# Clamping and scaling an MLP's h on VectorE straight from PSUM, and exponentials per head with bias and row sum

## The chip, the cores and the metric

One core of one Trainium2 chip runs the whole program. The metric is the device time of one execution in microseconds (us), the median of several runs. Engines: TensorE (PE, its weight loads are PEld), VectorE (DVE), ScalarE (ACT), GpSimd (POOL), and SyncE (SP), which issues the DMA transfers.

## What is computed

Three stages in float32, each feeding the next.

```python
# pooled attention: q, k, v are 8 x 8 x 576 x 64 (batch, heads, tokens, features)
k_p = k.reshape(B, H, 72, 8, D).mean(axis=3); v_p = ...      # 72 pooled keys and values
scores = q @ k_p.T / sqrt(D)
attn = exp(scores - max(scores)); attn = attn / (sum(attn) + 1e-09)
x = (attn @ v_p)  ->  4608 tokens x 512
# first MLP
h = x @ w_in                                                  # 512 -> 2048
g = where(h >= 1, h, where(h <= -1, 0, (h + 1)**2 / 4))
x = g @ w_out                                                 # 2048 -> 512
# second MLP: h = x @ w_in2; g = h * sigmoid(h); out = g @ w_out2
```

## The kernel before

Every product of the large matrices is made of float16 parts: an operand is scaled by a power of two and split into a high and a low half, and `three` (L119 to L122) issues the three products high x high, high x low and low x high into one PSUM bank. The scales are taken from the data while the program runs, so there are many operations of one column on DVE.

**The first MLP.** The 4608 tokens are 9 tiles of 512 (`NTILE`, `N`), the 2048 hidden features 16 chunks of 128 (`KF`). For a chunk, `emit_h` (twelve matmuls) makes h as 128 features x 512 tokens in one PSUM bank, `hps`. The pool `ps_h` has two banks; in the first tile four of every six chunks borrow one of the four `ps_y` banks instead. Four steps then make g:

- `pre_A` (L801, ACT): Relu of c1 x h + br from PSUM into an SBUF tile `g`
- `min_A` (L93 through the helper `ts`, DVE): the minimum of that with `lim`, into `u`
- `mid_A` (L808, ACT): the square of `u`, scaled
- `post_A` (L812, DVE): the larger of `g` - br and `u`, into `g`

`split_g` makes the halves for the next product: a cast on ACT (L840) and a subtraction on DVE (L841). The tiles `g` and `u` have three buffers each (`up`). `consts_A` works out c1, br, lim and the other factors of a tile from the scale of its x. The chunks of the weights (nine pieces, `cuts1`) have scales of their own, so c1 differs between pieces. `emit_yA` multiplies g with the second weight, three chunks behind h (`LAG`), into the four `ps_y` banks; `evac_yA` takes those out through ACT and DVE (L93 with `y`).

**The first tile is different.** Its 16 chunks of g are kept ("stash"), while the second weight W2 is still being converted in four column blocks: read as words and rebuilt in float32 on ACT and DVE (`xf`, L174 and others), its largest value found, scaled by a factor `ws` (ACT L207), cast (ACT L212), and the low half subtracted (POOL L213). Then all 16 chunks are multiplied with one column block after the other. The factor `ws` is computed on DVE. The looks at the first weight (L239, L240) stand in the same way ahead of the first h.

**The attention** runs in 36 tiles of 128 tokens, one tile ahead of the MLP. For a tile `att_qT` scales and splits the rows of q (mean L443, split L359 on ACT and L360 on DVE; the result is `rows`) and a DMA transposes them (`qT`). `att_scores` makes scores of 128 tokens x 8 heads x 72 keys in two PSUM banks (`att`, L542), four heads in each; then, half by half, DVE takes the maximum over 72 keys (L556) and subtracts it (L557) into an SBUF tile `e`, and one ACT instruction takes the exponential of all 576 columns (L561) with `scale` = `cq`, one number per token. The first four tiles run in float32 with a constant scale. `att_norm` sums e on DVE (L576), adds a small number (L577), takes the reciprocal (L580), multiplies on POOL (L581) and splits into halves. `att_T` transposes, and `att_pv` multiplies with the values and splits x (`xh`, `xl`). Keys and values are pooled by `kv_pool` on DVE (L438), eight sums for each batch of 576 tokens.

**What sets the order.** The source is written in the order of the loops shown below, with a chunk's parts one step behind each other. The order on each engine is then made by the Tile framework's scheduler, which simulates a timeline when the program is built; `paced` and `tc.issue_after` tie weight work to other instructions, and `tc.high_priority` draws the attention forward. So an edit in one place can move instructions elsewhere. Tiles of a pool are reused in turn: an instruction that writes one waits for the last reader of its former content.

The second MLP follows, from 957 us in the profile below, in blocks of 256 tokens with seven products instead of eight (`group_B`); the diff doesn't touch it.

## Time and profile before

| | |
|---|---|
| median of 3 runs | 1643.12 us (1642.25 to 1645.21) |
| profiled execution, span | 1642.1 us |
| instructions | 34714 |
| PE busy | 1552.3 us (95%) |
| DVE busy | 1267.9 us (77%) |
| ACT busy | 895.4 us (55%) |
| POOL busy | 536.1 us (33%) |

The profiled execution's own time is its span, 1642.1 us, 1.0 us under the median of the runs. Busy shares are means over the whole span. The program has stages: until the first h it loads and looks at weights; then the first tile without its second product; then the main loop; and at last the second MLP. So the share to look at is that of a stage, and for a wait the instruction that ends it.

### The profile page before, as it was taken

How to read it: one execution, taken by the hardware profiler on the slowest of the kernel's cores; microseconds unless marked ns; L12 is line 12 of the kernel's file. 1: busy time of each engine (PE TensorE's matmuls, PEld its weight loads, DVE VectorE, ACT ScalarE, POOL GpSimd, SP SyncE). 2: the span in 40 equal slices, each digit the busy share in tenths (PEclk: the TensorE clock that was granted, in tenths of full speed). 3: DMA queues.
4: the chain of work that ended last, by engine and by line, in shares of the span. 5: the costliest groups of instructions: out<-in, count | busy, mean ns of one | idle time of the engine just before them, and what ended most of it. 6: DMA issues, size and time to landing. Idle time of an engine off the chain costs nothing.

```text
span 1642.1 us, 34714 instructions
## 1 busy us (share of the span) xinstructions
PE 1552.3 (95%) x14406; PEld 1075.0 (65%) x14406; DVE 1267.9 (77%) x2208; ACT 895.4 (55%) x1420; POOL 536.1 (33%) x479
## 2 busy tenths in 40 slices
PE   6886799899999999999999999999999999999998
PEld 5642344444444444444444479999999999999998
DVE  6898887879888697887767667777677777777765
ACT  5477454665657557475656554555444554545543
POOL 2221512131323323231445423433343433343322
PEclk8687999999999999999999999999999999999999
DMA  9454468744445445357474330000100001000000
GB/s 292 117 172 101 104 152 219 175 107 123 133 114 152 87 129 127 77 140 213 156 298 136 147 129 28 27 28 28 40 27 27 28 33 35 27 27 28 27 15 27
DMA packets 217086, 166.36 MB, mean 101 GB/s; under 512 B 153952, under 2 KB 176480, under 8 KB 216928
## 3 DMA queue, kind: packets, MB, share of 16 engines
q1 hardware_dynamic: 216928, 164.14, 35.4%
q8 instruction: 113, 1.85, 0.5%
q14 instruction: 45, 0.37, 0.1%
HBM read 102.76 MB, written 33.55 MB: 83 GB/s over the span
## 4 chain that ended last, share of the span: by engine, by line
PE 40%; DVE 26%; issue 11%; ACT 9%; DMA 8%; POOL 6%; SPq 1%; DVEq 0%; ACTq 0%; POOLq 0%
DVE sum L438 5%; POOL c L702 4%; PE y L120 3%; PE y L122 3%; PE y L121 3%; PE y L1002 3%; PE y L1004 3%; PE y L1003 3%; PE hb L121 3%; PE hb L120 3%; PE hb L122 3%; PE hps L122 3%; PE hps L120 3%; PE hps L121 3%; DVE g L812 3%
## 5 line engine op out<-in xcount | busy, mean ns | idle before, releaser
L121 PE MATMUL hb<-xl,wc 128*128 128x128 f16 x2016 | 347.6, 219 | 0.0
L120 PE MATMUL hb<-xh,wc 128*128 128x128 f16 x2016 | 347.6, 219 | 0.0
L122 PE MATMUL hb<-xh,wc 128*128 128x128 f16 x2016 | 347.6, 219 | 0.0
L360 DVE SCALAR_TENSOR_TENSOR g<-c,tsg,g 128x512 f16<-128x512 f32 x252 | 228.6, 910 | 93.7 <-ACT g L359 93.7
L1002 PE MATMUL y<-wd,g 128*128 128x256 f16 x1008 | 274.7, 273 | 1.0 <-DVE ob L1015 1.0
L1003 PE MATMUL y<-wd,g 128*128 128x256 f16 x1008 | 274.7, 273 | 0.0
L1004 PE MATMUL y<-wd,g 128*128 128x256 f16 x1008 | 274.7, 273 | 0.0
L942 ACT ACTIVATE c<-c,tc 128x512 f32<-128x512 f32 x144 | 103.2, 717 | 229.8 <-DVE c L939 229.8
L359 ACT ACTIVATE g<-c,tsg 128x512 f16<-128x512 f32 x252 | 177.6, 718 | 85.7 <-POOL c L705 48.3
L120 PE MATMUL hps<-xh,wa 128*128 128x512 f16 x576 | 222.1, 386 | 2.2 <-ACT g L801 1.8
L120 PE MATMUL y<-g,wb 128*128 128x512 f16 x544 | 209.2, 387 | 15.6 <-ACT wb L212 11.5
L121 PE MATMUL hps<-xl,wa 128*128 128x512 f16 x576 | 221.8, 385 | 2.0 <-DVE skv L95 2.0
L122 PE MATMUL hps<-xh,wa 128*128 128x512 f16 x576 | 220.7, 384 | 0.0
L122 PE MATMUL y<-g,wb 128*128 128x512 f16 x544 | 210.2, 386 | 4.1 <-POOL wb L213 3.9
L121 PE MATMUL y<-g,wb 128*128 128x512 f16 x544 | 210.3, 386 | 0.7 <-DVE g L841 0.5
L939 DVE TENSOR_TENSOR c<-c,hb 128x512 f32<-128x512 f32 x252 | 168.0, 681 | 43.1 <-PE hb L122 40.9
L121 PEld LDWEIGHTS <-wc 128*128 128x128 f16 x2016 | 197.3, 98 | 2.4
L120 PEld LDWEIGHTS <-wc 128*128 128x128 f16 x2016 | 197.3, 98 | 2.2
L122 PEld LDWEIGHTS <-wc 128*128 128x128 f16 x2016 | 197.3, 98 | 0.0
L702 POOL TENSOR_TENSOR c<-c 128x512 f32<-128x512 f32 x108 | 164.0, 1532 | 2.8
L808 ACT ACTIVATE u<-u,trsg 128x512 f32<-128x512 f32 x144 | 103.3, 718 | 100.6 <-DVE u L93 100.4
L581 POOL TENSOR_TENSOR e<-e,den 128x576 f32<-128x576 f32 x36 | 44.4, 1237 | 348.2 <-DVE den L580 248.0
(185 smaller groups left out, 2802.4 us busy)
## 6 DMA issues: line engine op xcount, KB each, us to landing
raw<-in_moe_w_out_dram SPq DMA_DIRECT2D x21, 1024.0 KB
raw<-in_moe_w_in_dram SPq DMA_DIRECT2D x18, 1024.0 KB
raw<-in_v_dram SPq DMA_DIRECT2D x32, 288.0 KB
y<-y SPq DMA_DIRECT2D x36, 256.0 KB
yin<-y SPq DMA_DIRECT2D x18, 512.0 KB
out_dram<-ob SPq DMA_DIRECT2D x36, 256.0 KB
d<-hl SPq DMA_DIRECT2D x32, 256.0 KB
raw<-in_k_dram SPq DMA_DIRECT2D x28, 288.0 KB
```

The lines of the kernel that those rows point to most:

```text
L120: nc.tensor.matmul(out=acc, lhsT=wh, rhs=xh, start=start, stop=False)
L121: nc.tensor.matmul(out=acc, lhsT=wh, rhs=xl, start=False, stop=False)
L122: nc.tensor.matmul(out=acc, lhsT=wl, rhs=xh, start=False, stop=stop)
L359: a = nc.scalar.activation(out=hi, in_=x, func=AF.Copy, scale=s)
L360: return a, nc.vector.scalar_tensor_tensor(out=lo, in0=x, scalar=s, in1=hi, op0=ALU.mult, op1=ALU.subtract)
L702: nc.gpsimd.tensor_tensor(out=out, in0=a, in1=b, op=ALU.subtract)
L808: nc.scalar.activation(out=u_t[s], in_=u_t[s], func=AF.Square, scale=r["rsg"])
L939: nc.vector.tensor_tensor(out=out, in0=x, in1=y, op=ALU.add)
L942: nc.scalar.activation(out=x, in_=x, func=AF.Silu, scale=r["c1"])
L1002: nc.tensor.matmul(out=acc, lhsT=xh, rhs=wh, start=start, stop=False)
L1003: nc.tensor.matmul(out=acc, lhsT=xh, rhs=wl, start=False, stop=False)
L1004: nc.tensor.matmul(out=acc, lhsT=xl, rhs=wh, start=False, stop=stop)
```

## The change

Softmax: `att_scores` no longer subtracts. The maximum of a half is multiplied by -scale on DVE (two columns of four numbers each, a small `ts`), and ACT takes the exponential of each head's 72 columns straight from PSUM, with that product as `bias`, `scale` as before, and with `accum_out` writing the row's sum into `den`. There are eight such instructions for a tile where there was one. The sum on DVE in `att_norm` is gone.

First MLP: `pre_A` is now a DVE instruction that reads h from PSUM and clamps it between two numbers per partition, `lim` and its negative, which depend on the piece of the weight. `min_A` is gone. `mid_A` squares with a scale `cs` per piece and the bias `br`. `post_A` takes h from PSUM once more, multiplies it by c1 and takes the larger of that and the square. So ACT's Relu is gone, the two DVE instructions read PSUM, and the bank of h is read last by `post_A`, where before it was by `pre_A`. `consts_A` works out `cs`, `rs` and `lim` (18 columns) instead of `rsg` and a single `lim`.

```diff
--- before.py
+++ after.py
@@ -498,7 +498,7 @@
             done += n
         return r
 
-    q_t, qT_t, cq_t, at_t, aT_t, kT = {}, {}, {}, {}, {}, {}
+    q_t, qT_t, cq_t, at_t, aT_t, kT, den_t = {}, {}, {}, {}, {}, {}, {}
 
     def load_q(i):
         if i == NI - 1:
@@ -551,14 +551,17 @@
 
         e = at_t[i] = ap.tile([128, H, SP], F32, tag="e", name="e", bufs=2)
         mx = sm.tile([128, H], F32, tag="mx", name="mx")
+        den = den_t[i] = sm.tile([128, H], F32, tag="den", name="den")
+        scale = cq_t.pop(i, 1.0 / (POOL * D ** 0.5))
         for hf, sv in enumerate(halves):
             m4 = mx[:, 4 * hf:4 * hf + 4]
             nc.vector.tensor_reduce(out=m4, in_=sv, axis=AX.X, op=ALU.max)
-            nc.vector.tensor_tensor(
-                out=e[:, 4 * hf:4 * hf + 4], in0=sv, in1=m4.unsqueeze(2).to_broadcast([128, 4, SP]),
-                op=ALU.subtract,
-            )
-        nc.scalar.activation(out=e, in_=e, func=AF.Exp, scale=cq_t.pop(i, 1.0 / (POOL * D ** 0.5)))
+            ts(m4, m4, scale, -1.0, ALU.mult, ALU.mult)
+            for h in range(4 * hf, 4 * hf + 4):
+                nc.scalar.activation(
+                    out=e[:, h], in_=sv[:, h % 4], func=AF.Exp, scale=scale, bias=mx[:, h:h + 1],
+                    accum_out=den[:, h:h + 1],
+                )
 
     late = {}
 
@@ -572,8 +575,7 @@
 
     def att_norm(i):
         e = at_t[i]
-        den = sm.tile([128, H], F32, tag="den", name="den")
-        nc.vector.tensor_reduce(out=den, in_=e, axis=AX.X, op=ALU.add)
+        den = den_t.pop(i)
         nc.vector.tensor_scalar(
             out=den, in0=den, scalar1=1e-9, scalar2=2.0 ** -14, op0=ALU.add, op1=ALU.mult
         )
@@ -620,7 +622,8 @@
     def att_pv(i):
         t, j = divmod(i, NI)
         if j == 0:
-            r = XT[t] = small(e=1, s=1, sv=2, ch=len(cuts1), c1=len(cuts1), ge=1, sg=1, rsg=1, br=1, lim=1)
+            r = XT[t] = small(e=1, s=1, sv=2, ch=len(cuts1), c1=len(cuts1), cs=len(cuts1),
+                              lim=2 * len(cuts1), ge=1, sg=1, rs=1, br=1)
             r["x"] = new_x()
             x_scale(t, r)
         r = XT[t]
@@ -771,10 +774,13 @@
         ts(r["ge"], r["ge"], 4.0, op0=ALU.max)
         ts(r["ge"].bitcast(I32), r["ge"].bitcast(I32), 0x7F000000, op0=ALU.bitwise_and)
         bits(r["sg"], r["ge"], -1.0, 271)
-        bits(r["rsg"], r["ge"], 0.5, 55)
+        bits(r["rs"], r["ge"], -0.5, 199)
         ts(r["c1"], r["ch"], r["sg"], 0.5, ALU.mult, ALU.mult)
-        ts(r["br"], r["sg"], 0.25)
-        ts(r["lim"], r["sg"], 0.5)
+        ts(r["br"], r["rs"], 0.25)
+        ts(r["cs"], r["ch"], r["rs"], 0.5, ALU.mult, ALU.mult)
+        n = len(cuts1)
+        bits(r["lim"][:, 0:n], r["ch"], -1.0, 253)
+        ts(r["lim"][:, n:2 * n], r["lim"][:, 0:n], -1.0)
 
     acc_t = {}
     ydram = [dram.tile([128, KD, N], F32, name=f"y{t}") for t in range(NTILE)]
@@ -797,20 +803,19 @@
 
     def pre_A(s, r):
 
-        w = g32_t[s] = up.tile([128, N], F32, tag="g", name="g32")
-        nc.scalar.activation(out=w, in_=h_t.pop(s), func=AF.Relu, scale=c_A(r, "c1", s), bias=r["br"])
-
-    def min_A(s, r):
+        p = piece_of(cuts1, s % KF)
+        n = p + len(cuts1)
         u_t[s] = up.tile([128, N], F32, tag="u", name="u")
-        ts(u_t[s], g32_t[s], r["lim"], op0=ALU.min)
+        ts(u_t[s], h_t[s], r["lim"][:, p:p + 1], r["lim"][:, n:n + 1], ALU.min, ALU.max)
 
     def mid_A(s, r):
-        nc.scalar.activation(out=u_t[s], in_=u_t[s], func=AF.Square, scale=r["rsg"])
+        nc.scalar.activation(out=u_t[s], in_=u_t[s], func=AF.Square, scale=c_A(r, "cs", s), bias=r["br"])
 
     def post_A(s, r):
 
+        g32_t[s] = up.tile([128, N], F32, tag="g", name="g32")
         return nc.vector.scalar_tensor_tensor(
-            out=g32_t[s], in0=g32_t[s], scalar=r["br"], in1=u_t.pop(s), op0=ALU.subtract, op1=ALU.max
+            out=g32_t[s], in0=h_t.pop(s), scalar=c_A(r, "c1", s), in1=u_t.pop(s), op0=ALU.mult, op1=ALU.max
         )
 
 
@@ -1137,7 +1142,6 @@
         z = s - 1
         if 0 <= z < KF:
             pre_A(z, r)
-            min_A(z, r)
         if 1 <= z:
             split_g(z - 1, r)
         if 0 <= z < KF:
@@ -1187,7 +1191,6 @@
         z = s - 1
         if KF <= z < LAST:
             pre_A(z, XT[z // KF])
-            min_A(z, XT[z // KF])
         if KF + 1 <= z <= LAST:
             late["gl"] = split_g(z - 1, XT[(z - 1) // KF])
         if KF <= z < LAST:
```

The changed kernel's lines move by up to five: the maximum is L558, the exponential still L561, the small operation and the reciprocal on `den` are L579 and L582, the square is L812, the combining pass L817, the cast and the subtraction of the halves L845 and L846; the clamp is issued by `ts` at L95.

The scheduler's order moves with it. **DVE in the first tile, around the first scaled rows of q** (`rows`), that is between the chunk work of h (`u`, `g`, `stash`) and the constants of the second tile (`tsv`, `tge`, `tsg`, `tlim`). Before:

```order
L93 TENSOR_SCALAR u<-g_1175,tlim 128x512
L360 SCALAR_TENSOR_TENSOR rows<-qt,sq,rows 128x8x64
L95 TENSOR_SCALAR tsv<-ts,cols 128x1 x2
L93 TENSOR_SCALAR tge<-tge 128x1
L812 SCALAR_TENSOR_TENSOR g_1142<-g_1142,tbr,u 128x512
L841 TENSOR_TENSOR stash<-g_1121,stash 128x512
L93 TENSOR_SCALAR tge<-tge 128x1
L360 SCALAR_TENSOR_TENSOR v_115<-sum,skv,v_115 72x512
L812 SCALAR_TENSOR_TENSOR g_1175<-g_1175,tbr,u 128x512
L93 TENSOR_SCALAR eq<-eq 128x1
L95 TENSOR_SCALAR tsg<-tge 128x1
L95 TENSOR_SCALAR trsg<-tge 128x1
```

and now:

```order
L846 TENSOR_TENSOR stash<-g_1210,stash 128x512
L360 SCALAR_TENSOR_TENSOR v_115<-sum,skv,v_115 72x512
L95 TENSOR_SCALAR tsv<-ts,cols 128x1 x2
L95 TENSOR_SCALAR tlim<-tch 128x9
L93 TENSOR_SCALAR tge<-tge 128x1
L360 SCALAR_TENSOR_TENSOR rows<-qt,sq,rows 128x8x64 x2
L93 TENSOR_SCALAR tlim<-tlim 128x9
L93 TENSOR_SCALAR tge<-tge 128x1
L95 TENSOR_SCALAR tsg<-tge 128x1
L95 TENSOR_SCALAR trs<-tge 128x1
L95 TENSOR_SCALAR tc_1307<-tch,tsg 128x9
L93 TENSOR_SCALAR tbr<-trs 128x1
```

Before, a minimum, two combining passes and more chunk work stand among and behind the rows of q; now the last subtraction of the chunks (`stash`) and the split of v stand ahead of them, two tiles' rows stand together, and small operations follow.

**ACT in the first tile, at the second column block of W2** (`xf` is the block in float32, `wb_125` its high half). Before:

```order
L174 ACTIVATE xf<-raw 128x1024
L174 ACTIVATE xf<-wb_126 128x1024
L207 ACTIVATE xf<-xf,ws 128x1024 x2
L212 CAST wb_125<-xf 128x1024 x2
L561 ACTIVATE e<-e,cq 128x576
L359 ACTIVATE xh<-att,tsv 128x4x64
L174 ACTIVATE xf<-raw 128x1024
```

and now:

```order
L174 ACTIVATE xf<-raw 128x1024
L174 ACTIVATE xf<-wb_126 128x1024
L561 ACTIVATE e,den<-att,mx,cq 128x72 x4
L207 ACTIVATE xf<-xf,ws 128x1024 x2
L212 CAST wb_125<-xf 128x1024
L561 ACTIVATE e,den<-att,mx,cq 128x72 x4
L359 ACTIVATE xh<-att,tsv 128x4x64
L212 CAST wb_125<-xf 128x1024
```

Before, the scaling L207 and both casts stand in a row and the exponential behind them; now four exponentials stand ahead of the scaling, and four more with a split of x between the two casts.

**DVE in the main loop, where keys and values are pooled** (`sum<-raw`). Before:

```order
L557 TENSOR_TENSOR e<-att,mx 128x288
L812 SCALAR_TENSOR_TENSOR g_3631<-g_3631,tbr,u 128x512
L576 TENSOR_REDUCE den<-e 128x8
L577 TENSOR_SCALAR den<-den 128x8
L841 TENSOR_TENSOR g_3681<-g_3631,g_3681 128x512
L580 RECIPROCAL den<-den 128x8
L438 TENSOR_REDUCE sum<-raw 72x128 x4
L93 TENSOR_SCALAR u<-g_3677,tlim 128x512
L438 TENSOR_REDUCE sum<-raw 72x128 x2
L812 SCALAR_TENSOR_TENSOR g_3677<-g_3677,tbr,u 128x512
L438 TENSOR_REDUCE sum<-raw 72x128
L93 TENSOR_SCALAR u<-g_3742,tlim 128x512
```

and now:

```order
L558 TENSOR_REDUCE mx<-att 128x4 x2
L95 TENSOR_SCALAR mx<-mx,cq 128x4 x2
L817 SCALAR_TENSOR_TENSOR g_3711<-hps,tc_2131,u 128x512
L579 TENSOR_SCALAR den<-den 128x8
L582 RECIPROCAL den<-den 128x8
L438 TENSOR_REDUCE sum<-raw 72x128 x4
L846 TENSOR_TENSOR g_3750<-g_3711,g_3750 128x512
L95 TENSOR_SCALAR u<-hps,tlim 128x512
L438 TENSOR_REDUCE sum<-raw 72x128 x2
L95 TENSOR_SCALAR u<-hps,tlim 128x512
L438 TENSOR_REDUCE sum<-raw 72x128
L817 SCALAR_TENSOR_TENSOR g_3754<-hps,tc_2131,u 128x512
```

The sums of the keys stand in groups of four, two, one and one in both; the clamp of the next chunk now stands where the minimum did, behind four sums, and the combining pass that belongs to it comes after two more, another clamp, and one more sum.

## Rows read from the trace of the kernel before

**Rows 1.** Busy us of each engine by stage; columns: stretch, length, engines (instructions), PE clock, DMA share, GB/s

```profile
0.00:66.60 66.60, 47.69 (x293) 42.52 (x294) 45.88 (x98) 30.67 (x44) 12.48 (x18) 0.74 0.85 251
66.60:147.40 80.80, 57.79 (x301) 30.48 (x299) 77.30 (x139) 59.65 (x93) 19.75 (x10) 0.84 0.41 112
...
212.00:320.00 108.00, 97.62 (x608) 46.00 (x607) 87.67 (x191) 59.79 (x106) 12.59 (x13) 0.95 0.75 177
320.00:760.00 440.00, 428.15 (x2731) 204.06 (x2730) 362.14 (x680) 269.79 (x463) 125.59 (x130) 1.00 0.49 124
760.00:957.00 197.00, 188.43 (x978) 86.56 (x976) 139.97 (x198) 113.98 (x174) 82.90 (x81) 0.98 0.51 178
957.00:1642.00 685.00, 678.87 (x9136) 640.17 (x9134) 501.79 (x827) 332.27 (x503) 253.37 (x208) 1.00 0.10 35
```

**Rows 2.** Groups by line, first MLP; columns: out<-in count | busy us, mean ns | idle before, releaser

```profile
L812 DVE SCALAR_TENSOR_TENSOR g<-g,tbr,u 128x512 f32<-128x512 f32 x144 | 121.9, 847 | 46.8 <-ACT u L808 45.5
L801 ACT ACTIVATE g<-hps,tbr,tc 128x512 f32<-128x512 f32 x144 | 111.0, 771 | 48.1 <-PE hps L122 46.0 <-DVE g L841 2.0
...
L808 ACT ACTIVATE u<-u,trsg 128x512 f32<-128x512 f32 x144 | 103.3, 718 | 100.6 <-DVE u L93 100.4
...
L93 DVE TENSOR_SCALAR u<-g,tlim 128x512 f32<-128x512 f32 x144 | 86.3, 599 | 31.2 <-ACT g L801 30.8
...
L93 DVE TENSOR_SCALAR y<-y,cy 128x512 f32<-128x512 f32 x18 | 13.2, 740 | 1.0 <-PE y L122 0.9
```

**Rows 3.** The same view, attention and pooling

```profile
L438 DVE TENSOR_REDUCE sum<-raw 72x128 f32<-72x1024 f32 x48 | 89.4, 1909 | 0.0
...
L557 DVE TENSOR_TENSOR e<-att,mx 128x288 f32<-128x288 f32 x65 | 28.5, 447 | 0.2
...
L576 DVE TENSOR_REDUCE den<-e 128x8 f32<-128x576 f32 x36 | 26.8, 746 | 5.3 <-ACT e L561 5.3
...
L561 ACT ACTIVATE e<-e,cq 128x576 f32<-128x576 f32 x32 | 24.5, 765 | 3.1 <-DVE e L557 3.1
```

**Rows 4.** Line L93 between 320 and 900 us: duration ns, least/median/most

```profile
L93 DVE TENSOR_SCALAR u<-g,tlim x101: 434/478/1891, 324.3 to 896.1; 128x512 f32<-128x512 f32 x101
```

**Rows 5.** Timeline of ACT, a mean with its accumulator; columns: start us, us, instruction

```profile
126.17 0.62 ACT L443 ACTIVATE rows<-sum 72x512 f32<-72x512 f32 x1
126.69 0.19 ACT L443 ACTIVATION_READ_ACCUMULATOR rows<-sum 72x1 f32 x1
126.79 0.61 ACT L840 CAST stash<-g 128x512 f16<-128x512 f32 x1
```

**Rows 6.** Timeline of ACT at the start, the last early exponential

```profile
33.44 0.69 ACT L561 ACTIVATE e<-e 128x576 f32<-128x576 f32 x1 [0.32 <-DVE e L557]
```

**Rows 7.** Timelines of DVE, PE and ACT, from q's rows to W2; idle before in brackets

```profile
132.16 0.74 DVE L360 SCALAR_TENSOR_TENSOR rows<-qt,sq,rows 128x512 f16<-128x512 f32 x1
132.81 0.15 DVE L95 TENSOR_SCALAR ts<-te 128x1 int32<-128x1 int32 x1
...
143.50 0.68 DVE L841 TENSOR_TENSOR stash<-g,stash 128x512 f16<-128x512 f32 x1
...
135.75 1.17 PE L542 MATMUL att<-kT,qT 128*64 128x72 f16 x32 [5.47 <-DMA qT<-rows]
...
147.45 0.61 PE L120 MATMUL y<-g,wb 128*128 128x512 f16 x1 [6.73 <-ACT wb L212]
...
144.28 2.19 ACT L207 ACTIVATE xf<-xf,ws 128x1024 f32<-128x1024 f32 x2 [0.80 <-DVE ws L95]
```

**Rows 8.** Timeline of PE, the first matmuls with the second and third column block

```profile
166.06 0.39 PE L122 MATMUL y<-g,wb 128*128 128x512 f16 x1 [1.60 <-POOL wb L213]
...
183.55 0.61 PE L120 MATMUL y<-g,wb 128*128 128x512 f16 x1 [4.73 <-ACT wb L212]
```

**Rows 9.** Timeline of PE, two matmuls in a row in the main loop

```profile
372.70 0.38 PE L120 MATMUL hps<-xh,wa 128*128 128x512 f16 x1
372.92 0.38 PE L121 MATMUL hps<-xl,wa 128*128 128x512 f16 x1
```

## The prediction

> **What bounds the kernel now.** I read the busy times stage by stage first, because the change touches some stages only. From 957 us to the end PE is busy 679 of 685 us, and no changed line runs there: that 42% of the span can't move. In the two stages between 320 and 957 PE is busy 428 of 440 and 188 of 197 us: 20 us at most could be won there, and DVE, at 362 of 440, is not what holds PE. Before 320 it is different. Between 66.6 and 147.4 PE is busy 58 of 81 us, and DVE 77: this stage is VectorE's [rows 1]. So a DVE instruction saved or added counts in full there, and hardly at all later; and what ends that stage, the first use of the converted second weight, is a chain over DVE, ACT and POOL that I follow below.
>
> Then the costs by line. For each of the 144 chunks of 128 features ACT runs a Relu (771 ns) and a Square (718), DVE a min (mean 599) and a combining pass (847) [rows 2]. For each of 36 attention tiles DVE subtracts the maximum twice (447 each) and sums the row (746), and ACT makes one exponential of 576 columns (765) [rows 3].
>
> **The MLP part, per chunk.** The Relu goes: ACT saves 144 x 0.77 = 111 us, but ACT is not the bound in any stage of [rows 1] (60 of 81 us in the second), so I put this at nothing, and what hid it was DVE in the second stage and PE later. The min becomes a clamp that reads PSUM. The nearest row is the scaling of y out of PSUM, 740 ns, against a median of 478 for the min from SBUF [rows 2, 4]: +0.26 us each where nothing disturbs it. The combining pass now takes h from PSUM; with 740 as its price it loses 0.1 us of its mean. So undisturbed DVE gains nothing here: 144 x (0.74 + 0.74) = 213 us against 86 + 122 = 208.
>
> The means of the old forms are above their undisturbed times: 0.12 us x 144 = 17 us for the min (599 against the median 478), 0.11 x 144 = 15 us for the combining pass against 740. If the PSUM forms escape whatever stretches the others, that is what they save, and it is already in the 740. How far they escape is the bound: in the stage up to 147 the 16 clamps cost between -1 us (escaping, nothing else hit in their place) and +4.3 (16 x 0.26). I take +2, since another SBUF instruction is likely to stand where the stretched one stood.
>
> **The softmax part, per tile.** DVE loses 2 x 0.447 + 0.746 = 1.64 us and gets two small operations; some 1.2 us x 36 = 44 us less. ACT gets eight exponentials of 72 columns for one of 576. No row shows that form. The Relu has its operands (PSUM, scale and bias per partition), and the step from 512 to 576 columns of the one-pointer forms is 47 ns for 64 columns: 771 - 440 x 0.73 = 0.45 us [rows 2, 3]. A per-partition operand is worth about 718 - 610 = 0.11 (the Square against a plain cast of the same size) [rows 2, 5], so the four first tiles, whose scale is a constant, pay 0.34. The row sum adds a read of the accumulator; where one stands, an activation of 0.62 and its read of 0.19 together take 0.62 us from start to start [rows 5], so I put the pair at 0.45. Bounds: 0.34 and, without overlap, 0.64. Eight make 3.6 us (2.7 to 5.1) against 0.77, about +2.8 us on ACT a tile, so ACT's total stays about even.
>
> Where these 3.6 us stand is what decides. As the order shows, DVE's small den operation follows almost at once and waits for all eight, and everything on DVE stands behind it.
>
> **Start (to 66.6 us).** The exponentials of tiles 2 and 3 lie on ACT between the maxima and the last x split that DVE's weight maxima stand behind: before, the last ends at 33.44 + 0.69 [rows 6]. Each burst is 2.7 - 0.7 = 2.0 us longer, together 4; ACT's idle gaps (31 of 66.6 us busy) and the 1.6 us that DVE no longer spends there take part of it. Between 0 and 4 I take **+2**.
>
> **The stage up to the first second-layer product.** Before, the first split of q rows stands on DVE at 132.16, in the middle of the chunk work; nine chunk instructions follow it up to 143.50 (2 mins, 3 combining passes, 4 subtractions), and they hide the chain of rows, DMA transpose, scores, maximum, and the scale that W2 waits for. ACT's conversion starts at 144.28 and PE gets its weight at 147.45 [rows 7]. In the new order all chunk work stands ahead of those rows and nothing but small operations behind them. So the rows come at 132.2 + 2 (start) + 5.2 (two at 0.40, three at 0.66, four at 0.60: their durations less 0.08, by which the next begins early at 132.81) + 0.7 (the split of v, also moved ahead) + 2 (clamps) = 142. Behind them, uncovered: rows 0.74, transpose by DMA 2.85 (132.90 to 135.75), half of the scores 0.6, maximum and small operations about 1, four exponentials 1.8, one ACT pass over q 0.62, four more 1.8, a scaling 0.72, another pass 0.62: 10.7 us. ACT's conversion then starts at 152.7 and not 144.3: +8.4, of which 2 are the start's, so **+6.4**. The ends: +1 if the second burst and q's passes were done beforehand and the PSUM forms ran unstretched; +11 if the read of the sums does not overlap (8 x 0.19) and q's transpose takes some us more.
>
> **The three other column blocks of W2.** Before, ACT's conversion follows the scale at once; now four exponentials stand directly ahead of it, 1.8 us, and the subtraction that left (0.45) gives part back: +1.35 each. PE waits for the conversion in two of the three (1.6 and 4.7 us, at 166.06 and 183.55 [rows 8]): 2 x 1.35 = **+2.7** (0 to +6).
>
> **The main loop (212 to 957).** The change adds a wait: h's bank in PSUM is free only after clamp, Square and combining pass, not after the Relu. PE needs a chunk's two groups of twelve matmuls 24 x 0.216 = 5.2 us [rows 9], and with two banks the next but one h starts 7.8 us after an h has ended. Clamp, Square and pass are 0.74 + 0.72 + 0.74 = 2.2 us and some hand-overs; with a burst of 3.6 in between it is about 6. That fits. It is tight where DVE pools keys and values: eight reductions of 1.9 us [rows 3] at five places. There the new order puts four of them (7.6), a subtraction (0.6), a clamp (0.7), two (3.8), a clamp, one (1.9) and the pass (0.7) before a bank is free, 16 us; PE has in its queue till then two h, three y and the attention product, 13 to 14 us, plus what was under way. So it waits 1 to 3 us, where it lost at most 11.9 / 5 = 2.4 before (all idle of the 440 us stage, over five places) [rows 1]. DVE's den waits, some 2 to 3 us a tile, fall into DVE's spare time (78 of 440). **0**, from -8 to +10.
>
> Together +2 + 6.4 + 2.7 + 0 = +11.1. The profiled span is 1642.1 us, 1.0 under the median of 1643.1; I add the sum to the median: **1654**.
>
> **The rivals.**
> *Faster: DVE's relief reaches PE.* What the rows show: the min varies from 434 to 1891 ns [rows 4] and its mean is 0.12 above its median; 32 us of DVE are lost in both passes, and the softmax gives back 44. If most of PE's idle 10.4 + 11.9 + 8.6 = 31 us after 212 hangs on late DVE work, half of it, 15, goes, and ACT's idle time covers the bursts before: 1643 + 4 - 15 = 1632. It decides from the point where the stage up to 212 loses less than the loop gains. Against it: the loop's idle is spread over DMA transposes and ACT's means too, and the early chain is serial. The Trainium skill, SBUF — State Buffer, "Who interferes with whom", says that a DVE instruction with at most one SBUF input and outside the two-port modes does not contend with GpSimd, while one with two SBUF inputs does; by that rule both new PSUM forms escape, which is this rival's first half; the trace bears it out as far as 740 ns for the PSUM form goes. 0.22.
> *No change.* The scheduler's order hides more than I read from it: ACT passes over q done early, start absorbed, blocks a little better. 1643 +-3. 0.13.
> *Much slower: PSUM.* h's bank becomes PE's bound at the pooling places and behind bursts: 4 us more at each of the five and 0.5 us at each of 28 tiles, 34 less some 8 of the 11.9 now lost: 1654 + 26 = 1680; with half of it 1667. For it: the 16 us above; against: 7.8 us of room elsewhere. The skill's PSUM — Partial Sum Buffer, in "Summary: rules for kernel authors", says to evacuate promptly; this change does the opposite, and no row of before shows its price. 0.13.
> That the clamp doesn't replace the Relu as told is no rival: both read the same bank and the order shows it.
>
> **How the numbers follow.** My forecast has 0.52; its own range is 1645 to 1665. The range for 8 in 10, 1637 to 1669, leaves out about half of the faster rival and most of the much slower one. A measurement of this kernel tells 0.2% (3.3 us) from no change. Faster 0.22, same 0.13, slower 0.65.
>
> **What would show it.** Exponential plus read at about 0.45 us; clamp at 0.74 without long outliers; the first yA matmul at 155 to 157 us and not 147.5, the first hps at 68 to 69; the stage that begins with the main loop at 212 begins near 223; PE's busy time after 957 unchanged; in the loop a few waits of hps on DVE of 1 to 3 us behind poolings. I am wrong if the first yA comes before 150, or if PE's idle in the loop moves by more than 10 us.

## The result and the profile after

The changed kernel takes 1665.87 us (median of 4 runs, 1665.51 to 1666.08), the kernel before beside it 1642.68: a ratio of 1.0139, with a 95% interval of 1.0125 to 1.0154. That is 23 us slower. The forecast was 1654, so the direction is right and the size is half of what it is; 1666 lies near the upper end of the range. The profiled execution has a span of 1664.0 us against 1642.1.

The busy time of the engines by stage, in the changed kernel (columns as in [rows 1]). The cuts are the first h, the first product with W2, the second tile's first h and its second-layer product for the ninth of 16 chunks, and the end of the first MLP's products:

```profile
0.00:68.66 68.66, 49.69 (x292) 43.47 (x293) 41.22 (x96) 37.40 (x104) 12.10 (x18) 0.72 0.87 244
68.66:157.32 88.66, 55.31 (x301) 29.59 (x300) 80.00 (x144) 55.53 (x97) 17.95 (x12) 0.81 0.39 105
157.32:228.62 71.30, 56.81 (x368) 26.91 (x369) 47.96 (x75) 33.45 (x80) 26.41 (x18) 0.86 0.46 113
228.62:288.92 60.30, 57.87 (x368) 27.29 (x367) 48.32 (x109) 39.91 (x115) 11.73 (x13) 0.94 0.77 179
288.92:985.50 696.58, 665.32 (x3986) 313.83 (x3985) 532.22 (x948) 395.36 (x922) 199.59 (x215) 0.98 0.53 141
985.50:1664.00 678.50, 671.86 (x9097) 636.79 (x9095) 498.48 (x823) 330.93 (x500) 250.61 (x205) 1.00 0.10 34
```

The first h comes at 68.66 us and not 66.59 (+2.1), the first product with W2 at 157.32 and not 147.45 (+9.9). DVE is busy 80.00 us between the two, where it was 77.30 [rows 1]: still its stage. The four column blocks take 71.3 us and not 65.0, and the next stage is 4.7 us shorter (60.3 against 65.0). The kernel before in these two:

```profile
147.45:212.45 65.00, 53.85 (x368) 25.20 (x369) 53.59 (x80) 29.58 (x41) 29.44 (x20) 0.89 0.49 123
212.45:277.48 65.03, 60.17 (x354) 28.17 (x354) 49.85 (x115) 36.17 (x63) 10.46 (x10) 0.92 0.75 179
```

About half of the 4.7 us isn't won: PE is busy 2.3 us less in that stage, since the products of one chunk of h now lie behind its end. In the second MLP PE is idle for 6.6 us, before for 6.1 [rows 1].

So there are two losses: 9.9 us up to the first product with W2, and 12.0 behind it. The second one is best seen in one window from that product to the end, in which PE has the same matmuls in every kernel here. First the kernel before, then the changed one:

```profile
147.45:1642.10 1494.65, 1446.82 (x13814) 1001.99 (x13814) 1144.71 (x1972) 805.01 (x1284) 503.89 (x452) 0.99 0.33 94
```

```profile
157.32:1664.00 1506.68, 1451.84 (x13814) 1004.82 (x13814) 1126.99 (x1952) 799.65 (x1616) 488.35 (x450) 0.98 0.34 93
```

PE's idle time grows from 47.8 to 54.8 us (length less busy time), and the same 13814 matmuls take 5.0 us longer at a mean granted clock of 0.98 for 0.99. DVE is busy 18 us *less*, and ACT 5 less: neither is short of time over this window.

The groups of the changed lines (columns as in [rows 2]):

```profile
L812 ACT ACTIVATE u<-u,tbr,tcs 128x512 f32<-128x512 f32 x144 | 117.2, 814 | 161.1 <-DVE u L95 158.5 <-DVE cols L93 1.9 <-DVE den L579 0.3
L95 DVE TENSOR_SCALAR u<-hps,tlim 128x512 f32<-128x512 f32 x144 | 115.6, 803 | 27.3 <-PE hps L122 26.9
...
L817 DVE SCALAR_TENSOR_TENSOR g<-hps,tc,u 128x512 f32<-128x512 f32 x144 | 107.2, 745 | 50.1 <-ACT u L812 49.7
...
L561 ACT ACTIVATE e<-att,mx,cq 128x72 f32<-128x72 f32 x256 | 101.4, 413 | 26.1 <-DVE ws L95 15.6 <-DVE mx L95 9.3 <-PE att L638 0.3
...
L579 DVE TENSOR_SCALAR den<-den 128x8 f32<-128x8 f32 x36 | 8.6, 239 | 50.5 <-ACT e L561 50.4
```

The last row is the one to stop at. An operation with a mean of 0.24 us has 50.5 us of idle time in front of its 36 instances: DVE stands still until the eighth exponential has delivered its sum. In the kernel before its counterpart, the sum on DVE, waited 5.3 us [rows 3].

The timeline of DVE at one pooling place of the changed kernel, and PE's row that follows:

```profile
388.76 0.17 DVE L579 TENSOR_SCALAR den<-den 128x8 f32<-128x8 f32 x1 [2.56 <-ACT e L561]
388.97 0.20 DVE L582 RECIPROCAL den<-den 128x8 f32<-128x8 f32 x1
389.09 7.36 DVE L438 TENSOR_REDUCE sum<-raw 72x128 f32<-72x1024 f32 x4
396.36 0.69 DVE L846 TENSOR_TENSOR g<-g,g 128x512 f16<-128x512 f32 x1
396.95 0.81 DVE L95 TENSOR_SCALAR u<-hps,tlim 128x512 f32<-128x512 f32 x1
397.68 3.73 DVE L438 TENSOR_REDUCE sum<-raw 72x128 f32<-72x1024 f32 x2
401.31 0.81 DVE L95 TENSOR_SCALAR u<-hps,tlim 128x512 f32<-128x512 f32 x1
402.03 1.88 DVE L438 TENSOR_REDUCE sum<-raw 72x128 f32<-72x1024 f32 x1
403.83 0.75 DVE L817 SCALAR_TENSOR_TENSOR g<-hps,tc,u 128x512 f32<-128x512 f32 x1
...
404.63 0.38 PE L120 MATMUL hps<-xh,wa 128*128 128x512 f16 x1 [3.79 <-DVE g L817]
```

The wait for den (2.56), four poolings, a subtraction, a clamp, two poolings, a clamp, a pooling, and only then the combining pass that frees a bank of h. Over the whole program PE waits 26.3 us for this pass:

```profile
L120 PE MATMUL hps<-xh,wa 128*128 128x512 f16 x576 | 224.8, 391 | 26.5 <-DVE g L817 26.3
```

Five of these waits (5.61, 3.79, 3.84, 4.88 and 4.86 us, at 297, 404, 498, 615 and 712) are the pooling places. And such a wait is paid for twice. The windows around the third one, in the changed kernel (the last three numbers are granted clock, DMA share, GB/s):

```profile
493.00:498.50 5.50, 1.67 (x8) 0.68 (x7) 5.50 (x6) 0.90 (x3) 0.00 (x0) 0.97 0.65 175
498.50:503.00 4.50, 4.49 (x14) 1.75 (x14) 4.50 (x8) 1.23 (x2) 0.00 (x0) 0.66 0.46 131
503.00:508.00 5.00, 5.00 (x25) 2.25 (x24) 4.78 (x10) 3.57 (x6) 0.00 (x0) 1.00 0.05 11
```

After the 3.84 us in which PE stood still, the granted clock is 0.66 over the next 4.5 us, so part of that stretch ran at 1.2 and not 2.4 GHz, and 14 matmuls fill it; then it is 1.00 again. In the 4.5 us behind the waits of 5.61, 4.88 and 4.86 it is 0.70, 0.50 and 0.50; behind that of 3.79 it is 1.00. So the 5 us by which the same matmuls grew go with the longer waits.

### The profile page after: what moved, and what is told of

Same layout as the page of the kernel before. It is cut to its first block, busy times and chain, and to the rows that moved or that the text cites. A ratio compares the mean times of both kernels' runs of the same rounds, so it can differ in the third digit from the quotient of the medians.

```text
span 1664.0 us, 35111 instructions
## 1 busy us (share of the span) xinstructions
PE 1556.8 (94%) x14406; PEld 1077.9 (65%) x14406; DVE 1248.2 (75%) x2190; ACT 892.6 (54%) x1816; POOL 518.4 (31%) x479
## 4 chain that ended last, share of the span: by engine, by line
PE 51%; DVE 7%; ACT 4%; DMA 3%; issue 2%; POOL 2%; SPq 0%; DVEq 0%; ACTq 0%; POOLq 0%
PE hb L122 6%; PE hb L121 6%; PE hb L120 6%; PE y L1007 6%; PE y L1008 6%; PE y L1009 6%; PE hps L120 2%; PE hps L122 2%; PE hps L121 2%; PE y L120 2%; PE y L121 2%; PE y L122 2%; DVE sum L438 1%; ACT e L561 1%; DMA raw<-in_moe_w_out_dram 1%
## 5 line engine op out<-in xcount | busy, mean ns | idle before, releaser
L120 PE MATMUL hps<-xh,wa 128*128 128x512 f16 x576 | 224.8, 391 | 26.5 <-DVE g L817 26.3
L120 PE MATMUL y<-g,wb 128*128 128x512 f16 x544 | 204.2, 385 | 13.3 <-ACT wb L212 13.3
L122 PE MATMUL y<-g,wb 128*128 128x512 f16 x544 | 208.9, 385 | 5.9 <-POOL wb L213 5.9
L121 PE MATMUL y<-g,wb 128*128 128x512 f16 x544 | 209.0, 384 | 0.8 <-DVE g L846 0.8
L812 ACT ACTIVATE u<-u,tbr,tcs 128x512 f32<-128x512 f32 x144 | 117.2, 814 | 161.1 <-DVE u L95 158.5
```

What stands on the lines that cost most here:

```text
L120: nc.tensor.matmul(out=acc, lhsT=wh, rhs=xh, start=start, stop=False)
L121: nc.tensor.matmul(out=acc, lhsT=wh, rhs=xl, start=False, stop=False)
L122: nc.tensor.matmul(out=acc, lhsT=wl, rhs=xh, start=False, stop=stop)
L812: nc.scalar.activation(out=u_t[s], in_=u_t[s], func=AF.Square, scale=c_A(r, "cs", s), bias=r["br"])
```

## The experiments

The same points were read in each profiled execution. "First" is the first product with W2, "rest" the time from there to the end, "den" DVE's idle time ahead of its first operation on den over the whole program. A profiled execution's time is its span plus 1.8 us; where it lies 2 us or more off the median, the last column says so.

| kernel | median us | first | rest | den | profiled run off the median |
|---|---|---|---|---|---|
| before | 1642.68 (up to 1644.4 in later sets of runs) | 147.45 | 1494.65 | 5.3 | |
| changed | 1665.87 | 157.32 | 1506.68 | 50.5 | |
| e1 softmax part alone | 1665.26 | 150.96 | 1514.84 | 51.3 | +2.3 |
| e2 MLP part alone | 1653.69 | 149.64 | 1502.16 | 8.2 | |
| e3 old softmax in 8 tiles | 1656.40 | 150.28 | 1506.42 | 43.5 | +2.1 |
| e4 h copied by ACT | 1673.70 | 155.92 | 1515.78 | 53.3 | |
| e5 two exponentials, old MLP | 1641.71 | 148.37 | 1494.33 | 8.7 | +2.8 |
| e6 two exponentials, new MLP | 1652.35 | 151.77 | 1500.33 | 19.8 | |
| e7 poolings cut, before | 1629.60 | 146.49 | 1481.21 | 4.2 | one run |
| e8 poolings cut, changed | 1646.31 | 156.27 | 1488.23 | 50.7 | one run |
| e9 four exponentials, old MLP | 1641.65 | 147.36 | 1492.44 | 13.6 | |
| e10 eight without sums, old MLP | 1660.19 | 147.12 | 1509.08 | 30.3 | -2.2 |
| e11 changed, no den operations | 1656.04 | 157.32 | 1493.58 | none | -3.1 |
| e12 two exponentials, late tiles | 1642.52 | 145.30 | 1494.60 | 7.8 | |
| e13 softmax alone, no den operations | 1654.86 | 151.46 | 1501.34 | none | |
| e14 poolings paced by the maximum | 1662.73 | 157.13 | 1505.97 | 33.4 | +2.4 |

**The parts one by one (e1 to e3).** e1 undoes the MLP hunks, e2 the softmax hunks, and e3 keeps the old softmax for the first eight attention tiles:

```diff
             m4 = mx[:, 4 * hf:4 * hf + 4]
             nc.vector.tensor_reduce(out=m4, in_=sv, axis=AX.X, op=ALU.max)
+            if not (i >= 2 * NI):
+                nc.vector.tensor_tensor(
+                    out=e[:, 4 * hf:4 * hf + 4], in0=sv, in1=m4.unsqueeze(2).to_broadcast([128, 4, SP]),
+                    op=ALU.subtract,
+                )
+                continue
...
+        if not (i >= 2 * NI):
+            nc.scalar.activation(out=e, in_=e, func=AF.Exp, scale=scale)
...
+        if not (i >= 2 * NI):
+            nc.vector.tensor_reduce(out=den, in_=e, axis=AX.X, op=ALU.add)
```

> Only the softmax part of the change; the first MLP is as before (Relu on ACT, minimum, Square, combining pass from SBUF). Theory A (the exponentials' bursts on ACT cost the time up to the end of the first tile, h's bank held by the combining pass costs the main loop): first h at 68.7 us (+2), the four column blocks of W2 take 70 to 72 us as in the changed kernel (71.3) and not 65.0, and the main loop has no wait of PE for the combining pass and takes 745 to 750 us as before (747.6); 1651 to 1660 us in all. Theory B (the MLP part costs the early time by moving chunk work ahead of q's rows, and the exponentials are hidden): first h at 66.6 to 67, blocks 65 to 66, under 1648 us.

> Only the MLP part of the change; the softmax is as before. Theory A: first h at 66.6 us, the stage of the chunks shorter by some 7 us as in the changed kernel, the first second-layer product at 147 to 150, blocks 65 us, and in the main loop five waits of PE for the combining pass of 4 to 6 us each, the loop 752 to 755 us; 1647 to 1653 us in all. Theory B: the first second-layer product at 154 or later, 1656 us or more.

> The changed kernel, but the first eight attention tiles (four at the start, four during W2's conversion) have the old softmax. Theory A: up to the main loop as with the MLP part alone (first h at 66.6, blocks 65), then the loop of the changed kernel (753 us, five waits for the combining pass): 1647 to 1653 us. Theory B: the early time stays as in the changed kernel, 1660 us or more. If the 28 later tiles' bursts cost the loop something by themselves, this run is slower than the MLP part alone by that much; theory A says by less than 2 us.

Measured: 1665.26 (ratio 1.0138, 1.0120 to 1.0157), 1653.69 (1.0063, 1.0043 to 1.0083) and 1656.40 (1.0078, 1.0056 to 1.0099). The theory I began with placed the delay of the first h well: with the softmax alone it comes at 68.78, with the MLP alone at 65.53. From there to the first product with W2 neither part explains the change: 80.9 us before, 82.2 with the softmax alone, 84.1 with the MLP alone, and 88.6 to 88.8 in all five kernels that have both with eight exponentials throughout. And the theory was wrong for the loop. The softmax alone, which leaves h's banks as they were, loses 20.2 us behind the first product with W2, 8.7 of them in the column blocks and 11.5 behind; it should have lost nothing in the loop.

The MLP alone loses 7.5 us behind that product, although DVE stands only 8.2 us for den in it. PE's row in that run and the window (columns as in [rows 2] and [rows 1]):

```profile
L120 PE MATMUL hps<-xh,wa 128*128 128x512 f16 x576 | 222.7, 387 | 22.3 <-DVE g L827 22.0 <-ACT xh L359 0.4
```

```profile
149.64:1651.80 1502.16, 1449.47 (x13814) 1003.23 (x13814) 1161.37 (x1983) 728.50 (x1154) 494.36 (x452) 0.99 0.34 94
```

So the late release of h's bank costs something by itself: at the five pooling places PE waits 2.5 to 4.3 us for the combining pass (4 to 6 expected), and DVE has 17 us more work than before in the window. With this MLP the later 28 tiles' bursts add 2.7 us (e3 against e2, where under 2 was expected; the two intervals overlap): 35 us more of standing for den, against 28 us less of work on DVE. The parts don't add up: 21 and 10 us alone, 22 together.

**Is it h's bank (e4)?** From the second tile on ACT copies c1 x h to SBUF, and the combining pass reads the copy:

```diff
+        if s >= KF:
+            g32_t[s] = up.tile([128, N], F32, tag="g", name="g32")
+            nc.scalar.activation(out=g32_t[s], in_=h_t[s], func=AF.Copy, scale=c_A(r, "c1", s))
...
+        if s >= KF:
+            return nc.vector.tensor_tensor(out=g32_t[s], in0=g32_t[s], in1=u_t.pop(s), op=ALU.max)
```

> The changed kernel, but from the second tile on ACT also copies c1 x h to SBUF, and the combining pass reads that copy, so that h's bank is free after the clamp and the copy. Theory A (the last read holds the bank): the five waits of PE for the combining pass of 3.8 to 5.6 us each go or fall under 1.5 us, the main loop takes 742 to 749 us and the whole 1654 to 1661. Rival C (the clamp on DVE holds the bank just as long, since it stands behind the same poolings): the waits stay at 3 us or more, now for the clamp, and the loop at 752 or more; 1663 to 1668 us.

PE's waits with the copy (columns as in [rows 2]):

```profile
L120 PE MATMUL hps<-xh,wa 128*128 128x512 f16 x576 | 222.2, 386 | 9.2 <-DVE u L95 7.7 <-ACT xh L359 1.5
...
L120 PE MATMUL y<-g,wb 128*128 128x512 f16 x544 | 201.9, 387 | 23.2 <-ACT wb L212 13.6 <-ACT g L850 8.1 <-DVE y L93 1.5
```

The waits for the combining pass went as expected, and the time rose by 8 us all the same, to 1673.70: PE waits for g's cast on ACT instead (8.1 us), and ACT has 872 us of work where it had 800 in the same window. An early release of the bank, bought with ACT time, is no gain. The run shows what replaced the waits; it doesn't show what a free early release would be worth.

**The length of the burst (e5, e6, e9, e10, e12).** A shift that is the same for a whole row drops out of the softmax. So one maximum may serve two or four heads, with fewer and longer exponentials, the row sums again on DVE:

```diff
+            nc.vector.tensor_reduce(out=mx[:, hf:hf + 1], in_=sv, axis=AX.XY, op=ALU.max)
+            ts(mx[:, hf:hf + 1], mx[:, hf:hf + 1], scale, -1.0, ALU.mult, ALU.mult)
+            nc.scalar.activation(
+                out=e[:, 4 * hf:4 * hf + 4], in_=sv, func=AF.Exp, scale=scale, bias=mx[:, hf:hf + 1],
+            )
```

e9 has two maxima and two exponentials of 144 columns for a half; e10 has the change's eight, without `accum_out`; e12 uses two from the ninth tile on.

> The kernel before with another softmax: per half of four heads one maximum over all four, and one exponential of 288 columns straight from PSUM with it as bias (a shift that is the same within a row of a head drops out of the softmax); the row sums on DVE as before, no subtraction. So the exponentials read PSUM as in the change, but a tile has two of some 0.5 us and no accumulator reads. The first MLP is as before. Theory D (the length of the burst of eight, 3.1 us, is what costs, ahead of W2's scaling and ahead of DVE's operation on den): four column blocks 65 to 67 us, main loop within 3 us of before, 1637 to 1646 us in all. Rival F (it is the hand-over: scores held in PSUM till ACT has read them, so that the next matmuls with an attention bank wait for ACT): blocks 70 us or more, the loop 5 to 10 us longer as with the softmax part alone, 1655 or more.

> The changed kernel with the softmax of the run before (two exponentials of 288 columns, row sums on DVE); the MLP part is that of the change. Theory D: like the MLP part alone, 1645 to 1654 us, with main-loop waits for the combining pass of 2.5 to 4 us and not 4 to 6. Rival F: as the changed kernel, 1660 us or more.

> The kernel before with four exponentials of 144 columns for a tile, straight from PSUM with one maximum for two heads each as bias, row sums on DVE; the first MLP as before. Theory D (the time that a tile's exponentials take on ACT in a row is the cost): between two exponentials (1641.7 us) and the softmax part alone (eight with sums, 1665.3), 1645 to 1656 us. Rival F (reading scores from PSUM on ACT costs as such, or the sums do): 1640 to 1644 like two, or 1660 and more like eight.

> The softmax part alone with its eight exponentials, but without accum_out: the row sums are made on DVE as before. Eight at 0.30 us from start to start are 2.4 us and not 3.1, and DVE has its 0.75 us back for the sum. Theory D: 1653 to 1663 us. Rival H (the accumulator's read and the wait for its eight results are what costs): 1640 to 1648 us.

> The kernel before, with two exponentials for a tile from the ninth attention tile on and the old softmax in the first eight; the first MLP as before. If the two exponentials cost nothing by themselves in the main loop and save DVE its subtractions, the first second-layer product stays at 147 to 148 us and the rest takes 1489 to 1494: 1636 to 1642 us. If the gain of that form is nothing, 1642 to 1645.

With the old MLP, two, four and eight exponentials and eight with sums give 1641.71, 1641.65, 1660.19 and 1665.26 us. Two are no different from the kernel before (0.9987, 0.9973 to 1.0002; the column blocks take 68.5 us, 65 to 67 expected), nor are four (0.9994, 0.9985 to 1.0003), which I had expected at 1645 or more; eight without sums is 1.0105 (1.0090 to 1.0121). It is no straight line in the exponentials' time on ACT. The den column has the same order, 8.7, 13.6, 30.3 and 51.3 us of DVE standing still, but the time isn't in proportion to it either: the step from 13.6 to 30.3 costs 18.5 us, that from 30.3 to 51.3 another 5.1, 3.8 of them ahead of the first product with W2. Reading scores from PSUM on ACT costs nothing that the time shows with two or four exponentials, so the rival of the hand-over fell. With the new MLP two exponentials give 1652.35 (e6), as expected like the MLP part alone. Its waits for the combining pass are 0.8 to 2.6 us, shorter than expected; but at the first pooling place PE waits 5.17 us there, put down to an operation of one column on DVE. e12 is as fast as the kernel before (0.9992, 0.9983 to 1.0001): no version here that does the whole work is faster than the kernel before beyond the noise.

**The poolings (e7, e8).** DVE sums one of eight tokens from the third batch on, in both kernels:

```diff
-            nc.vector.tensor_reduce(out=dst, in_=r.rearrange("p h r d -> p h d r"), axis=AX.X, op=ALU.add)
+            n = POOL if b < 2 else 1
+            nc.vector.tensor_reduce(out=dst, in_=r[:, :, 0:n].rearrange("p h r d -> p h d r"), axis=AX.X, op=ALU.add)
```

> The kernel before, but from the third batch on the keys and values that DVE pools are summed over one of the eight tokens only (seven eighths of that sum are left out), so that a pooling takes some 0.3 us and not 1.9. Its partner is the next run, and the loop from the first product of the second tile to that of the eighth is compared (before: 563.9 us, changed kernel: 577.7). Theory D (DVE's series of poolings, with the wait for den in front, is where PE runs dry): this loop falls to 545 to 558, PE's waits at the five places go.

> The changed kernel with the same poolings cut to one of eight tokens. Theory D: PE's waits for the combining pass fall under 1 us each, and the loop between the same points is less than 4 us longer than in the run before (it was 13.8 longer with the poolings whole). Rival G (the bursts on ACT and the late release of h's bank cost in every tile, poolings or not): the loop stays 9 us or more longer.

In the window that I had named, which runs from the second tile's ninth chunk to the eighth's and not from first product to first product, the lengths are 548.0 and 562.3: 14.3 apart, not under 4, though PE has the same products of h and y in both. So theory D missed by its own measure, and rival G's 9 or more came. PE's waits for the combining pass don't all fall under 1 us either: there are six, up to 2.73 us, 8.2 in all. Over the rest the difference does fall, from 12.0 to 7.0 us, since e8 is 7.3 us shorter than e7 outside that window. These are single runs, and single runs of the kernel before lie up to 6 us from their median, so how much of the 12 us hangs on the poolings isn't shown; by either measure more than half of it stays without them.

**The wait for den (e11, e13, e14).** In e11 and e13 DVE's two operations on den are gone and POOL multiplies by the sum as it is; the eight exponentials stay as they are on ACT. The poolings are then paced by the scaled maximum. e14 keeps the operations on den and has only this other pace. The two hunks of e11 and e13, the first of them also in e14:

```diff
-            ts(m4, m4, scale, -1.0, ALU.mult, ALU.mult)
+            late["dve"] = nc.vector.tensor_scalar(
+                out=m4, in0=m4, scalar1=scale, scalar2=-1.0, op0=ALU.mult, op1=ALU.mult
+            )
...
-        nc.vector.tensor_scalar(
-            out=den, in0=den, scalar1=1e-9, scalar2=2.0 ** -14, op0=ALU.add, op1=ALU.mult
-        )
-        late["dve"] = nc.vector.reciprocal(out=den, in_=den)
```

> The changed kernel without DVE's two small operations on den: POOL multiplies the exponentials by their sum as it is (the reciprocal is left out), so that the eight exponentials stay as they are on ACT, and nothing on DVE waits for them. The poolings are paced by the scaled maximum in place of the reciprocal. From the first second-layer product to the end the changed kernel takes 1506.7 us, the kernel before 1494.7, the MLP part alone 1502.2. Theory D1 (DVE's wait of some 2.5 us for den ahead of the poolings): at most 1502, and waits of PE for the combining pass under 3.5 us each. Rival D2 (ACT is held up by its own bursts, whoever waits for den): 1505 or more.

> The softmax part alone (first MLP as before) without DVE's two small operations on den: POOL multiplies by the sum as it is (the reciprocal is left out), and the poolings are paced by the scaled maximum. From the first second-layer product to the end the softmax part alone takes 1514.8 us, the kernel before 1494.7, and DVE stands still for den for 45.9 and 5.3 us there. Theory D1 (DVE's standing still for den is the cost of this part): 1500 or less, 1645 to 1652 us in all, though the bursts on ACT are the same. Rival D2 (the bursts hold up ACT's own Relus, Squares and casts, which are all there in this kernel): 1508 or more, over 1657 in all.

> The changed kernel with its operations on den, only that the poolings are paced by the scaled maximum and no longer by the reciprocal, so that DVE has poolings to do while the eight exponentials run, at those places. From the first second-layer product to the end the changed kernel takes 1506.7 us. If the run without den waits was faster because the waits stand ahead of the poolings: 1494 to 1502, with PE's waits for the combining pass at 1.5 to 3.2 us at the pooling places, 1653 to 1661 us in all. If it was because of all the den waits, those in other places too: 1503 to 1507, 1662 to 1666 in all.

e11 takes 1656.04 us (ratio 1.0075, 1.0060 to 1.0089), 9.8 less than the changed kernel, with the first product with W2 at the same 157.32. The window from there to the end:

```profile
157.32:1650.90 1493.58, 1447.36 (x13814) 1003.50 (x13814) 1117.84 (x1890) 799.02 (x1616) 485.38 (x450) 0.99 0.34 94
```

```profile
L120 PE MATMUL hps<-xh,wa 128*128 128x512 f16 x576 | 221.4, 385 | 18.2 <-DVE g L815 17.2 <-DVE eq L93 0.7
```

ACT is as busy as in the changed kernel (799.0 and 799.7 us), h's bank is still read last by the combining pass, for which PE waits 17.2 us and not 26.3, and the rest is as short as before the change, 1493.6 (1496.7 if set against its median). The waits at the pooling places are 1.7 to 3.1 us. The same third wait, at 489, is 1.67 us here, and the windows around it show no fall of the clock:

```profile
484.00:489.40 5.40, 3.74 (x19) 1.77 (x17) 5.40 (x5) 0.68 (x3) 0.00 (x0) 1.00 0.78 179
489.40:493.90 4.50, 4.49 (x21) 2.05 (x21) 4.03 (x9) 2.50 (x4) 0.00 (x0) 1.00 0.34 95
```

21 matmuls in the 4.5 us in which the changed kernel has 14. e13 (1654.86; 1.0070, 1.0047 to 1.0094) gives 10.4 us back to the softmax alone, about half of its loss. Its rest, 1501.3, and its time lie between what the theory (1500 or less, 1645 to 1652) and the rival (1508 or more, over 1657) had named, and the rest is 6.7 above the kernel before: with the Relus still on ACT, something of the loss stays without any wait for den. That it is the bursts holding up ACT is likely and not shown. e14 (1662.73; 1.0122, 1.0095 to 1.0150) brings the waits at the pooling places to 1.2 to 3.2 us and gives back only 3.1 us, with an interval that overlaps that of the changed kernel (1.0125 to 1.0154): DVE still stands 33.4 us for den. So what e11 gives back doesn't come from the order at the pooling places alone; about a third does.

Two things stay open. Without the two operations DVE also saves their own 16 us (8.6 and 7.2 us busy), and these runs don't part that from the waiting. The price of DVE's work in e7 speaks for the waiting: 71 us of it left out of the kernel before gave 13.4 us in the rest, so 16 us would be worth some 3, an estimate from a single run. And den waits aren't the whole loss, since the MLP alone loses 7.5 us nearly without them; what the late release of the bank is worth beside the bursts no run shows.

## Why the prediction was half right

- **The start, +2: right in size.** The first h is at 68.66 (+2.1), with the softmax alone +2.2, with the MLP alone not later. Single profiles are no finer than that: kernels with the old softmax in the first tiles have it at 64.3 to 66.6, those with eight exponentials and their sums at 67.2 to 68.8. Eight without sums (e10) are at 66.07, so that the longer bursts alone do it isn't borne out.
- **Up to the first product with W2: right in its steps, a little short, and the point at which the scaling starts partly by luck.** The chain was forecast and came in the order told: rows of q, DMA, scores, exponentials, scaling. The timelines of PE, and of DVE and ACT:

```profile
144.13 1.17 PE L542 MATMUL att<-kT,qT 128*64 128x72 f16 x32 [14.78 <-DMA qT<-rows]
148.13 0.80 PE L107 MATMUL all<-ident,wm 128*128 128x128 f32 x2 [2.82 <-ACT e L561]
157.32 0.61 PE L120 MATMUL y<-g,wb 128*128 128x512 f16 x1 [8.40 <-ACT wb L212]
...
140.09 1.40 DVE L360 SCALAR_TENSOR_TENSOR rows<-qt,sq,rows 128x512 f16<-128x512 f32 x2
...
152.25 0.63 ACT L443 ACTIVATE rows<-qt 128x512 f32<-128x512 f32 x1 [1.39 <-DMA qT<-rows]
152.79 0.19 ACT L443 ACTIVATION_READ_ACCUMULATOR rows<-qt 128x1 f32 x1
152.88 2.17 ACT L207 ACTIVATE xf<-xf,ws 128x1024 f32<-128x1024 f32 x2
154.96 0.75 ACT L588 CAST e<-e 128x288 f16<-128x288 f32 x2
155.61 0.72 ACT L359 ACTIVATE rows<-qt,sq 128x512 f16<-128x512 f32 x1
```

  The scores come 8.4 us later than in [rows 7], ACT's scaling of W2 starts at 152.88 (forecast 152.7), and PE's product at 157.32 (155 to 157 forecast). Two errors cancel in the 152.7: the rows start at 140.1 and not 142, and what stands behind them takes 12.8 us and not 10.7, 1.4 of it a mean on ACT that waits for the DMA of the next rows. Behind the scaling, two casts of e and a split now stand ahead of W2's cast, 1.3 us that weren't forecast. The second row of PE is a step I left out: the product for W2's maximum needs an attention bank, and that is now free only when the exponentials have read it. It did no harm beyond the chain.
- **The column blocks, +2.7: too small, and in part given back.** Only the burst ahead of the scaling was counted. ACT's timeline at the second block shows two:

```profile
170.38 0.41 ACT L561 ACTIVATE e<-att,mx,cq 128x72 f32<-128x72 f32 x1 [7.64 <-DVE ws L95]
170.69 0.19 ACT L561 ACTIVATION_READ_ACCUMULATOR e<-att,mx,cq 128x1 f32 x1
170.79 0.40 ACT L561 ACTIVATE e<-att,mx,cq 128x72 f32<-128x72 f32 x1
...
171.95 2.19 ACT L207 ACTIVATE xf<-xf,ws 128x1024 f32<-128x1024 f32 x2
174.03 1.04 ACT L212 CAST wb<-xf 128x1024 f16<-128x1024 f32 x1
174.96 0.42 ACT L561 ACTIVATE e<-att,mx,cq 128x72 f32<-128x72 f32 x1
...
176.88 1.07 ACT L212 CAST wb<-xf 128x1024 f16<-128x1024 f32 x1
```

  The second one, with a split, stands between the two casts and holds up the second by 1.9 us; the order quoted with the change had it in plain sight. The blocks grew by 6.3 us, and the next stage shrank by 4.7, 2.3 of them work that moved behind its end. So up to there it came to +1.6, or about +3.9 for the same work.
- **The main loop, 0: the step that failed.** It put DVE's waits for den into "DVE's spare time (78 of 440)". DVE does have that time on average, but a wait is not taken from the average: it stands ahead of poolings, clamps and combining passes that PE needs next. 36 tiles x 1.4 us = 50.5 us of waiting, 45 of them behind the first product with W2; without the operations that wait, the changed kernel is 9.8 us faster. From the second tile's ninth chunk to the end it costs 1664.0 - 288.92 = 1375.1 against 1642.1 - 277.48 = 1364.6 us, +10.5, or about +8 for the same work. The other half of the zero, the late release of h's bank, was put at nothing too, and with the MLP alone it goes with 22.0 us of PE's waits and 7.5 us of time. Nor had the sum a term for the clock: over the whole window from the first product with W2, 7.0 of the 12.0 us are more idle time of PE and 5.0 are the same matmuls taking longer. So the sign that I had named, PE's idle time moving by more than 10 us, did not show.
- **PE's waits at the pooling places, 1 to 3 us: measured 3.8 to 5.6.** Without the operations on den they are 1.7 to 3.1 (e11), which is what was worked out; with the MLP alone, which has no burst, 2.5 to 4.3. So the order was read rightly, and the larger part of what was left out is the 2.6 us ahead of it, with the lower clock behind it.
- **The Relu that leaves ACT, valued at nothing: wrong beside the bursts.** With no den waits in either, the rest is 1501.3 with the Relus (e13) and 1493.6 without (e11; 1496.7 against its median), although the MLP part makes DVE's work longer. With the old softmax the same part costs 7.5 us. That fits with the two parts together costing no more than the softmax alone.
- **Prices.** An exponential and its read take 0.39 us from start to start (four from 170.38 to 171.95; taken at 0.45), a clamp 0.803 (0.74), a combining pass 0.745 (0.74). The longest clamp is 0.818 us and the longest combining pass 0.759; of the old form, one took 2.03 in the main loop. The PSUM forms do escape what stretches the others. In the trace of before each of the 24 combining passes over 0.9 us and of the 19 minima over 0.7 us runs beside an instruction of POOL, and so do 20 and 21 of the shorter ones. The Trainium skill, SBUF — State Buffer, "Who interferes with whom", says that DVE instructions with at most one SBUF input, outside the two-port modes, do not contend with GpSimd, and the trace agrees, with 0.759 at most for the new pass. It brought nothing that the time shows.
- **The rivals.** The faster one had its first half right and lost to the early chain and the waits. "Much slower: PSUM" came nearest in number (1667 with half of its price) and had the place right, and half of the mechanism: PE does wait for the last reader of the bank, 22.0 us with the MLP alone and 26.3 in the changed kernel, but freeing the bank earlier by a copy on ACT made it slower (e4), and taking the operations on den out brought the loop's time back with the late release left in place (e11). The Trainium skill, PSUM — Partial Sum Buffer, "Summary: rules for kernel authors", asks to evacuate promptly; the 26.3 us that PE waits for the last reader agree, and e4 shows that here it wasn't worth an extra pass on a busy engine.

## What to carry to other kernels

An instruction that needs the last of a burst of small ones on another engine blocks its own engine for the whole burst, whatever it costs itself: look at the idle time in front of small operations, and at what is queued behind them. Spare time of an engine as a mean doesn't hide a wait; other work ahead of it in the queue can shorten it, as in e14, where DVE stood 17 us less for a gain of about 3 us. And before a long operation is split to save a pass elsewhere, try the split in two: here, with the old MLP, two or four exponentials were free, and eight were not.

## What the runs showed of the hardware

Reading the accumulator costs ACT little: a record of 0.19 to 0.23 us adds 0.09 from start to start (0.39 with it, 0.30 without: in e10 four exponentials of 0.41 us take 1.32 together). The cost of a short activation is mostly fixed: 413 ns for 72 columns, 465 for 144 and 582 for 288 in the groups of the changed kernel, e9 and e5. A clamp from PSUM with two bounds per partition takes 0.803 us, against 0.740 for a scaling with one factor. The granted clock behind a wait of PE isn't told by the wait's length alone: it fell to 0.50 to 0.70 behind four waits of 3.84 to 5.61 us in the changed kernel and not behind one of 3.79, in e11 it fell behind waits of 3.00 and 3.02 us and not behind one of 3.07, and in e6 behind waits of 2.63 and 2.64.
